# A Fourier-mixing and gated-MLP kernel: the skipped branch without SyncE and VectorE, the last output unit in two halves, and four smaller moves

## The chip, the core and the metric

The kernel runs on one core of a Trainium2 chip. The metric is the device time of one execution in microseconds (us), less is better. The core has five engines that run their own instruction streams and meet at semaphores: TensorE (PE in the profile; PEld are its weight loads), VectorE (DVE), ScalarE (ACT), GpSimd (POOL) and SyncE (SP). SyncE and GpSimd issue DMAs here, which 16 DMA engines carry out.

## What is computed

A token mixing by a two-dimensional Fourier transform and a gated MLP, both of the same x (2048 tokens of 512), are mixed by a sigmoid gate:

```python
def reference(A_x, A_dft_seq_re, A_dft_seq_im, A_dft_hid_re, A_dft_hid_im, B_x, B_w1, B_w3, B_w2, gate_w):
    x = A_x
    g = sigmoid((x * gate_w).sum(-1, keepdims=True))
    a = x @ dft_hid_re.T ;  b = x @ dft_hid_im.T           # over the 512 hidden columns
    y = dft_seq_re @ a - dft_seq_im @ b                    # over the 2048 tokens
    h = silu(x @ w1) * (x @ w3)                            # F = 1376
    return g * y + (1 - g) * (h @ w2)
```

All data are float32. The four DFT matrices are inputs like any other.

## The kernel before

**Arithmetic.** Each float32 operand is split into a high and a low part of a reduced float32 type, and a product is three matmuls (high x high, high x low, low x high; helper at L128). The splits are `high` on ScalarE (L114) and `low` on VectorE (L117).

**Order.** The order is written out by hand: each engine runs its instructions in the order of the code, and a semaphore is waited for where data come from another engine. SyncE's DMAs go out in code order too, one queue over eight semaphore lanes (HW0 to HW7) taken in turn.

**Stages.** After a start of 5.8 us come the gate and up products (to about 207 us): 22 items, each a chunk of 128 of the F columns for one half of the tokens, each item 7 products of 42 matmuls in all (PSUM tiles X, Z and Y; weights `wa` and `wb`). The summed weights `wb` of a chunk are made once, written to DRAM (`wbsp`) and read back by SyncE in two halves ahead of each use (`load_wb`, L206, tiles named wb0_n and wb1_n for weight set n). Then the products with w2 (H, about 207 to 321 us), and the Fourier part in a folded form (321 us to the end). The folded form holds if the DFT matrices have the symmetries of a DFT, and it needs sums and differences of blocks of x ("folds").

**Background tasks.** The folds and the test of the symmetries run beside the products on ScalarE and VectorE. They are tasks in a list; calls of `work` at fixed places of the product loop issue those whose turn it is, by costs that are written beside them, and `load_ahead` issues their loads on SyncE's queue as long as buffers are free. `load_pair` (L661) loads two blocks of x, xr0 and xr7 first. To compare the matrices, blocks `t` of a DFT matrix (16 in each of four groups O1a, O1b, O2, E2) are loaded by SyncE (L728), VectorE takes the difference to a representative block (`differ`, L733 and L735, 128x1024) and ScalarE sums the absolute values (`add_up`, L744). `lone` loads three small pieces with SyncE (L942 to L944) and does some 30 small sums on GpSimd.

**The end.** The Fourier part makes the forms O1, O2 and E2 in PSUM; `even` (L1289) splits each half of E2 into `z_E`, in two pieces of 258 columns for ScalarE and two for VectorE. Then come ten units Y0 to Y9 (L1301). A unit is 12 matmuls into one PSUM tile (6 for the even columns, 128x258, and 6 for the odd ones, 128x256; `chain_two`, L1281), for Y0 to Y5 two updates and for Y6 to Y9 one update of VectorE that reads the tile, scales by the gate and adds the MLP part (L1324, tile r), and one DMA on SyncE's queue to the output (L1325). Units 6 to 9 each give 128 rows of the output.

**The flag and the skipped path.** After unit 3 the sums of the comparison are tested (`verdict`), a matmul of one column adds the 128 results up (`sum_flags`, L576, in front of unit 6), VectorE turns the sum into a flag in SBUF (`see_flags`, L579, behind unit 6's update), and each engine loads the flag into a register (SyncE at L1338, the four others at L1340 behind unit 9). A branch on that register (`tc.If`, L1347) skips a block that computes the Fourier part without any symmetry. With the inputs used here the block is always skipped. An engine that has instructions in the block jumps over them and then, in the else side, brings its semaphores to the values that the block would have left; an engine without instructions in it has nothing to make up. At the end (L1587) SyncE checks its queues' semaphores one by one, drains, and the engines meet at a barrier.

Of the kernel before, what the change touches and what calls it, by code (L numbers as in the profile page):

```python
# [10 lines left out]
AF = mybir.ActivationFunctionType  # L11
# [19 lines left out]
def fnet_swiglu_gate_kernel(  # L31
# [26 lines left out]
    nc = tc.nc  # L58
# [529 lines left out]

    COLD, LAND, TOKENS, RATE, HOLD = [], [4], [1.0], [0.7], [4]
# [11 lines left out]
    def load_ahead(n):  # L601
        thaw()
        for i in ORDER:
            _, _, _, _, f, need, temps = QUEUE[i]
            if i in LOADED:
                continue
            if sum(k not in ISSUED and QUEUE[k][5] > 0 for k in LOADED) >= n or len(F4) < need + temps + min(HELD_BACK[0], HOLD[0]) + RES[0]:
                return
            if f and TOKENS[0] < 0:
                return  # L610
            if f:
                f()
                TOKENS[0] -= need
            HELD_BACK[0] += temps
            LOADED[i] = NOW[0] if f else -99
# [114 lines left out]
    def differ(kind, i):  # L730
        t, r = TR[16 * GROUPS.index(kind) + i], REP[kind]
        if i < 8:
            nc.vector.tensor_sub(t, t, r)  # L733
        elif kind != "E2":
            nc.vector.tensor_add(t, t, r)  # L735
        else:
            im = i > 11
            tv = t.rearrange("p (k n) -> p k n", k=2)
            nc.vector.tensor_tensor(tv, tv, r[:, None, 512 * im : 512 * im + 512].to_broadcast([P, 2, 512]),
                                    op=ALU.add if im else ALU.subtract)  # L740
# [193 lines left out]
    def lone():  # L934
# [7 lines left out]
        nc.sync.dma_start(r0[:1], edges[:, :1024])  # L942
        nc.sync.dma_start(four[:1], edges[:, 1024:1028])
        nc.sync.dma_start(spc, misc[:, :32])  # L944
# [73 lines left out]
    for n in range(SPARE[0], NI):  # L1018
# [5 lines left out]
        do(at_end, n, work, "A", 0.0 if ITEMS[min(n + LOOK, NI - 1)] == (NC - 1, 1) else 1.2)  # L1024
    do(at_end, SPARE[1] - 2, lambda: LIMIT.__setitem__(0, n_gate))
# [263 lines left out]
    def even(p):  # L1289
# [4 lines left out]
        at = [slice(258 * v, 258 * v + 258) for v in range(2)]  # L1294
        for v in range(2):
            high(z[:, 0, at[v]], ps[v])
        for v in range(2):
            low(z[:, 0, at[v]], z[:, 1, at[v]], ps[v])

    even(0)  # L1300
    for u, (kind, za, zb, n, swap) in enumerate(UNITS):  # L1301
# [3 lines left out]
        if u == 6:  # L1305
            sum_flags(ps)

# [3 lines left out]
        evens, odds = (ps[:, lo:hi].rearrange("p (n a) -> p n a", a=2) for lo, hi in ((254, 512), (512, 768)))  # L1311
        chain_two(evens, [(zs(0, za), of_d(0, 0)), (zs(1, zb), of_d(1, 0))])
        chain_two(odds, [(zs(1, za), of_d(0, 1)), (zs(0, zb), of_d(1, 1))])
        r = yp.tile([P, 1024], F32, tag=f"r{u % 6}", name=f"r{u}")
# [5 lines left out]
        for i in range(n):  # L1320
# [3 lines left out]
            nc.vector.scalar_tensor_tensor(rv, src, g_pos[:, k : k + 1], nv, op0=ALU.mult, op1=ALU.add)  # L1324
        nc.sync.dma_start(out[FIRST[u] : FIRST[u] + n].rearrange("k p n -> p k n"),  # L1325
# [10 lines left out]
        if u == 6:  # L1336
            see_flags(ps)
            nc.sync.reg_load(bad_in[mybir.EngineType.SP], seen)  # L1338
    for e in (nc.gpsimd, nc.scalar, nc.tensor, nc.vector):
        e.reg_load(bad_in[e.engine], seen)  # L1340
# [6 lines left out]
    with tc.If(bad > 0, label="other"):  # L1347
# [11 lines left out]
        for q in range(8):  # L1359
            nc.sync.dma_start(xa[q], xs[q])  # L1360
        for k in range(4):
            nc.sync.dma_start(da[k], df[k])
        for b in range(NTB):
            two = [pair_of(k, f"all{b}_{k}") for k in range(4)]
            uv = [[two[2 * v + m // 2][:, 512 * (m % 2) : 512 * (m % 2) + 512] for m in range(4)] for v in range(2)]
            for q in range(8):
                for par in range(2):
                    c = get(pair, "c", 1024)
                    nc.sync.dma_start(c, wf[b, q, par])
# [10 lines left out]
            for j in range(TB // P):  # L1380
# [9 lines left out]
                else:  # L1390
                    nc.sync.dma_start(nb, nbsp[k - 8])
                nc.vector.scalar_tensor_tensor(y, ps, g_pos[:, k : k + 1], nb, op0=ALU.mult, op1=ALU.add)
                nc.sync.dma_start(out[k], y)
# [200 lines left out]
```

## Time and profile before

| | before |
|---|---|
| runs | 356.77, 357.47 and 358.74 us, median 357.47 us |
| the profiled execution | 357.24 us, of it 355.3 us span from the first to the last instruction |
| mean granted TensorE clock | 0.994 |
| busy: TensorE, VectorE, ScalarE, GpSimd | 348.3 (98%), 308.6 (87%), 233.8 (66%), 67.6 us (19%) |
| DMA | 103.04 MB, mean 290 GB/s |

The span is what the profile's times count from; the rest of the time, 1.9 us, lies around it. In a row of the profile, "out<-in" gives the tiles without their numbers, "x7" the count, the number behind a comma the mean of one in ns, and the bracket or the last column how long the engine idled just before and for what. A q behind an engine's name (SPq, POOLq) marks what its sequencer does beside computing: DMA issues, register loads, branches, semaphore checks.

### The profile page before, as it was taken

What the parts mean: (1) busy time and instruction counts of PE and PEld (TensorE: products, weight loads), DVE (VectorE), ACT (ScalarE), POOL (GpSimd) and SP (SyncE); (2) the same over time, 40 slices, a digit from 0 to 9 for tenths busy, and PEclk for the clock granted to TensorE, in tenths of its full rate; (3) what the DMA queues carried; (4) which work ended last, traced back from release to release, by engine and by line L of the source; (5) the groups of instructions that cost most, each with busy time, mean ns of one, the idle gap of its engine ahead of it and who ended that gap; (6) DMA issues with size and microseconds to landing.
All of it is one profiled execution on the core that took longest, in us unless ns stands there. A gap on an engine that the chain in (4) does not pass through costs nothing.

```text
span 355.3 us, 5132 instructions
## 1 busy us (share of the span) xinstructions
PE 348.3 (98%) x1720; PEld 304.5 (86%) x1720; DVE 308.6 (87%) x418; ACT 233.8 (66%) x395; POOL 67.6 (19%) x118
## 2 busy tenths in 40 slices
PE   8999999999999999999999999999999999999993
PEld 4888888888888888888888888888888888889992
DVE  4999989999869788888887799989969979998982
ACT  5875766556648687775433589552588998879930
POOL 0012333333101222111112843421021010000000
PEclk9999999999999999999999999999999999999997
DMA  7648995669636779999999159996659999998184
GB/s 286 245 160 293 351 367 215 221 235 343 214 121 220 213 226 396 400 402 401 365 389 285 52 157 385 406 355 220 223 164 395 404 410 408 409 409 315 59 316 163
DMA packets 33861, 103.04 MB, mean 290 GB/s; under 512 B 5925, under 2 KB 6183, under 8 KB 33832
## 3 DMA queue, kind: packets, MB, share of 16 engines
q1 hardware_dynamic: 26344, 75.93, 57.7%
q0 software_dynamic: 7488, 26.75, 20.3%
q8 instruction: 14, 0.23, 0.3%
q14 instruction: 15, 0.12, 0.1%
HBM read 78.02 MB, written 24.65 MB: 289 GB/s over the span
## 4 chain that ended last, share of the span: by engine, by line
PE 97%; DMA 1%; DVE 0%; issue 0%
PE H L128 32%; PE X L128 31%; PE Z L128 15%; PE Y L128 8%; PE C L128 3%; PE Y L1281 3%; PE O L128 3%; PE wps L416 1%; PE E L128 1%; DMA out<-r 1%; DVE r L1324 0%; PE Y L576 0%
## 5 line engine op out<-in xcount | busy, mean ns | idle before, releaser
L128 PE MATMUL H<-w2t,ht 128*128 128x512 f32 (+1 forms) x528 | 114.1, 379 | 0.0
L128 PEld LDWEIGHTS H<-w2t,ht 128*128 128x128 f32 (+1 forms) x528 | 99.8, 189 | 14.2
L128 PE MATMUL X<-xo,wb 128*128 128x512 f32 x378 | 88.6, 379 | 0.0
L128 PEld LDWEIGHTS X<-xo,wb 128*128 128x128 f32 x378 | 71.4, 189 | 10.2
L744 ACT ACTIVATE t<-t 128x1024 f32<-128x1024 f32 (+1 forms) x68 | 67.4, 994 | 1.5 <-DVE t L733 1.4
L319 POOL DMA_DIRECT2D hs<-h x36 | 19.7, 547 | 88.2 <-DVE h L390 63.4
L401 ACT ACTIVATE h<-X 128x512 f32<-128x512 f32 x21 | 12.5, 596 | 32.0 <-PE X L128 29.9
L733 DVE TENSOR_TENSOR t<-t,rep 128x1024 f32<-128x1024 f32 x28 | 33.1, 1219 | 0.0
L114 ACT ACTIVATE ht<-hr 128x1024 fp32r<-128x1024 f32 x19 | 20.0, 1053 | 18.3 <-PE H L128 10.6
L380 DVE TENSOR_TENSOR u<-u,X 128x512 f32<-128x512 f32 x21 | 14.4, 687 | 20.1 <-PE X L128 12.1
L128 PE MATMUL X<-xo,wa 128*128 128x512 f32 x126 | 30.7, 380 | 0.0
L128 PE MATMUL Z<-xo,wa 128*128 128x512 f32 x126 | 30.6, 379 | 0.0
L128 PE MATMUL Y<-xo,wa 128*128 128x512 f32 x126 | 30.6, 379 | 0.0
L128 PE MATMUL Z<-xo,wb 128*128 128x512 f32 x126 | 30.6, 379 | 0.0
L735 DVE TENSOR_TENSOR t<-t,rep 128x1024 f32<-128x1024 f32 x24 | 28.2, 1219 | 0.0
L128 PEld LDWEIGHTS X<-xo,wa 128*128 128x128 f32 x126 | 23.7, 189 | 3.6 <-DVE wa L117 0.3
L128 PEld LDWEIGHTS Y<-xo,wa 128*128 128x128 f32 x126 | 23.8, 189 | 3.4
L128 PEld LDWEIGHTS Z<-xo,wb 128*128 128x128 f32 x126 | 23.8, 189 | 3.4
L128 PEld LDWEIGHTS Z<-xo,wa 128*128 128x128 f32 x126 | 23.8, 189 | 3.4
L117 DVE TENSOR_TENSOR ht<-hr,ht 128x1024 fp32r<-128x1024 f32 x19 | 23.2, 1219 | 0.1
L117 DVE TENSOR_TENSOR wa<-ws,wa 128x768 fp32r<-128x768 f32 (+1 forms) x22 | 19.3, 880 | 4.0 <-ACT wa L114 3.8
L114 ACT ACTIVATE wa<-ws 128x768 fp32r<-128x768 f32 (+2 forms) x21 | 16.9, 806 | 7.8 <-PE Z L128 6.0
(197 smaller groups left out, 492.5 us busy)
## 6 DMA issues: line engine op xcount, KB each, us to landing
t<-wt SPq DMA_DIRECT2D x60, 512.0 KB, 9.2
hr<-hs SPq DMA_DIRECT2D x19, 512.0 KB, 7.4
hs<-h POOLq DMA_DIRECT2D x36, 256.0 KB, 5.2
wbsp<-wb POOLq DMA_DIRECT2D x16, 512.0 KB, 4.5
wb<-wbsp SPq DMA_DIRECT2D x16, 512.0 KB, 9.5
xs_B<-xt SPq DMA_DIRECT2D x8, 512.0 KB, 3.9
xr<-xw SPq DMA_DIRECT2D x8, 512.0 KB, 13.0
ws<-w POOLq DMA_DIRECT2D x6, 512.0 KB, 5.0
```

Of the source, the lines that this page charges most:

```text
L114: nc.scalar.activation(hi, src, AF.Copy)
L117: nc.vector.tensor_sub(lo, src, hi.bitcast(F32))
L128: nc.tensor.matmul(ps.rearrange("p (n a) -> p n a", a=2), u, turns(v)[:, some], **kw)
L319: nc.gpsimd.dma_start(hs[c][:, b * TB : (b + 1) * TB], h)
L380: nc.vector.tensor_add(u4, u4, x)
L401: nc.scalar.activation(g1, x, AF.Silu)
L416: nc.tensor.matmul(wps, warm[:, :P], warm, start=True, stop=True)
L733: nc.vector.tensor_sub(t, t, r)
L735: nc.vector.tensor_add(t, t, r)
L744: nc.scalar.activation(t[:, :n], t[:, :n], AF.Abs, accum_out=acc[:, i : i + 1])
L1281: nc.tensor.matmul(to, u[i], v[j], start=n == k == 0, stop=n == len(terms) - 1 and k == 2, skip_group_check=True)
```

## The change

- **Skipped path.** In the skipped block, the DMAs go from SyncE to GpSimd's queue, and the last update from VectorE to ScalarE (scaling) and GpSimd (addition). SyncE and VectorE have no instruction left in it.
- **Last unit in halves.** Unit 9's odd columns get a PSUM tile of their own, `Yodd`; its update and its output DMA are done in two halves of 128x256.
- **Flag sooner.** The flag's matmul stands in front of unit 5, `see_flags` in front of unit 5's updates, and SyncE, GpSimd and ScalarE load the register there; TensorE loads it in front of unit 8, VectorE still at the end.
- **O2's differences.** The block differences of group O2 are two VectorE instructions of 128x512 instead of one of 128x1024.
- **Folds of x.** With `PAUSE`, `load_ahead` issues no background load from the middle to the end of the one item in which xr0 and xr7 would be first, so that a load of `wb` goes out ahead of them.
- **Small loads.** The three DMAs of `lone` move to GpSimd's queue.
- **E2's splits** are one piece of 516 columns for each engine and half.

```diff
--- before.py
+++ after.py
@@ -586,6 +586,7 @@
         ORDER.append(len(QUEUE) - 1)
         return ORDER[-1]
 
+    PAUSE = [False]
     COLD, LAND, TOKENS, RATE, HOLD = [], [4], [1.0], [0.7], [4]
 
     def free_later(*tiles):
@@ -600,6 +601,8 @@
 
     def load_ahead(n):
         thaw()
+        if PAUSE[0]:
+            return
         for i in ORDER:
             _, _, _, _, f, need, temps = QUEUE[i]
             if i in LOADED:
@@ -729,7 +732,11 @@
 
     def differ(kind, i):
         t, r = TR[16 * GROUPS.index(kind) + i], REP[kind]
-        if i < 8:
+        if kind == "O2":
+            f = nc.vector.tensor_sub if i < 8 else nc.vector.tensor_add
+            for a in range(2):
+                f(*(v[:, 512 * a : 512 * a + 512] for v in (t, t, r)))
+        elif i < 8:
             nc.vector.tensor_sub(t, t, r)
         elif kind != "E2":
             nc.vector.tensor_add(t, t, r)
@@ -939,9 +946,9 @@
         r0, r1 = ROWS
         for v in (edge_p, er_p):
             g.memset(v.bitcast(F32), 0.0)
-        nc.sync.dma_start(r0[:1], edges[:, :1024])
-        nc.sync.dma_start(four[:1], edges[:, 1024:1028])
-        nc.sync.dma_start(spc, misc[:, :32])
+        nc.gpsimd.dma_start(r0[:1], edges[:, :1024])
+        nc.gpsimd.dma_start(four[:1], edges[:, 1024:1028])
+        nc.gpsimd.dma_start(spc, misc[:, :32])
         a, b = r0[:1, :512], r0[:1, 512:]
         u, v = r1[:1, :512], r1[:1, 512:]
         g.tensor_add(u, a, b)
@@ -1022,6 +1029,8 @@
             do(mid, n, work, "D", 1.7 if n >= SPARE[1] else 1.3 if WSET[n] == WSET[n + 1] else 0.0)
         do(second, n, work, "A", 2.4 if n < NI - 1 else 0.0)
         do(at_end, n, work, "A", 0.0 if ITEMS[min(n + LOOK, NI - 1)] == (NC - 1, 1) else 1.2)
+    do(mid, SPARE[1], PAUSE.__setitem__, 0, True)
+    do(at_end, SPARE[1], PAUSE.__setitem__, 0, False)
     do(at_end, SPARE[1] - 2, lambda: LIMIT.__setitem__(0, n_gate))
 
 
@@ -1291,37 +1300,51 @@
         ps = two[:, :258], two[:, 512:770]
         forms(*ps, ("E2",), range(2), p)
         z = Z["E2", p] = z_E[:, p]
-        at = [slice(258 * v, 258 * v + 258) for v in range(2)]
-        for v in range(2):
-            high(z[:, 0, at[v]], ps[v])
-        for v in range(2):
-            low(z[:, 0, at[v]], z[:, 1, at[v]], ps[v])
+        zh, zl = (z[:, h].rearrange("p (v n) -> p v n", v=2) for h in range(2))
+        split(zh, zl, two.rearrange("p (v n) -> p v n", v=2)[:, :, :258])
 
     even(0)
     for u, (kind, za, zb, n, swap) in enumerate(UNITS):
         if u == 4:
             even(1)
         ps = next_two(f"Y{u}")
-        if u == 6:
+        if u == 5:
             sum_flags(ps)
+        if u == 8:
+            nc.tensor.reg_load(bad_in[mybir.EngineType.PE], seen)
 
         def zs(p, at):
             return [Z[kind, p][:, h, at : at + P] for h in range(2)]
 
-        evens, odds = (ps[:, lo:hi].rearrange("p (n a) -> p n a", a=2) for lo, hi in ((254, 512), (512, 768)))
+        apart = u == len(UNITS) - 1
+        po = next_two("Yodd") if apart else ps
+        evens, odds = (v[:, lo:hi].rearrange("p (n a) -> p n a", a=2)
+                       for v, lo, hi in ((ps, 254, 512), (po, 512, 768)))
         chain_two(evens, [(zs(0, za), of_d(0, 0)), (zs(1, zb), of_d(1, 0))])
         chain_two(odds, [(zs(1, za), of_d(0, 1)), (zs(0, zb), of_d(1, 1))])
+        if u == 5:
+            see_flags(ps)
+            for e in (nc.sync, nc.gpsimd, nc.scalar):
+                e.reg_load(bad_in[e.engine], seen)
         r = yp.tile([P, 1024], F32, tag=f"r{u % 6}", name=f"r{u}")
         nb = NB.pop(u)
 
         def both(v):
             return v.rearrange("p (a m) -> p a m", a=2)[:, :, :256]
 
-        for i in range(n):
+        for i in range(0 if apart else n):
             k = FIRST[u] + i
             rv, nv = (both(v[:, i * D : i * D + D]) for v in (r, nb))
             src = both(ps[:, 255:769])[:, :, ::-1] if i ^ swap else both(ps[:, 254:770])
             nc.vector.scalar_tensor_tensor(rv, src, g_pos[:, k : k + 1], nv, op0=ALU.mult, op1=ALU.add)
+        if apart:
+            k = FIRST[u]
+            for a, src in enumerate((ps[:, 255:511], po[:, 512:768])):
+                at = slice(256 * a, 256 * a + 256)
+                nc.vector.scalar_tensor_tensor(r[:, at], src[:, ::-1], g_pos[:, k : k + 1], nb[:, at],
+                                               op0=ALU.mult, op1=ALU.add)
+                nc.sync.dma_start(out[k][:, at], r[:, at])
+            continue
         nc.sync.dma_start(out[FIRST[u] : FIRST[u] + n].rearrange("k p n -> p k n"),
                           r.rearrange("p (k n) -> p k n", k=2)[:, :n])
         if FIRST[u] > 7:
@@ -1333,11 +1356,7 @@
             work_until(set(range(n_late)))
         if u == 3:
             verdict()
-        if u == 6:
-            see_flags(ps)
-            nc.sync.reg_load(bad_in[mybir.EngineType.SP], seen)
-    for e in (nc.gpsimd, nc.scalar, nc.tensor, nc.vector):
-        e.reg_load(bad_in[e.engine], seen)
+    nc.vector.reg_load(bad_in[mybir.EngineType.DVE], seen)
     bad = nc.snap(bad_in, donate=True, min_val=0, max_val=0x3F800000)
     close(zo_a_cm, lp_cm)
     close(mov_cm, sp_cm, hh_cm, f4d_cm, y_cm)
@@ -1357,16 +1376,16 @@
         xa = [get(gen, f"x{q}", 1024) for q in range(8)]
         da = [get(gen, f"d{k}", 1024) for k in range(4)]
         for q in range(8):
-            nc.sync.dma_start(xa[q], xs[q])
+            nc.gpsimd.dma_start(xa[q], xs[q])
         for k in range(4):
-            nc.sync.dma_start(da[k], df[k])
+            nc.gpsimd.dma_start(da[k], df[k])
         for b in range(NTB):
             two = [pair_of(k, f"all{b}_{k}") for k in range(4)]
             uv = [[two[2 * v + m // 2][:, 512 * (m % 2) : 512 * (m % 2) + 512] for m in range(4)] for v in range(2)]
             for q in range(8):
                 for par in range(2):
                     c = get(pair, "c", 1024)
-                    nc.sync.dma_start(c, wf[b, q, par])
+                    nc.gpsimd.dma_start(c, wf[b, q, par])
                     for v in range(2):
                         for m in range(4):
                             sl = slice(par * D + m * P, par * D + m * P + P)
@@ -1388,9 +1407,10 @@
                 if k < 8:
                     nb = NBK[k // 2][:, k % 2 * D : (k % 2 + 1) * D]
                 else:
-                    nc.sync.dma_start(nb, nbsp[k - 8])
-                nc.vector.scalar_tensor_tensor(y, ps, g_pos[:, k : k + 1], nb, op0=ALU.mult, op1=ALU.add)
-                nc.sync.dma_start(out[k], y)
+                    nc.gpsimd.dma_start(nb, nbsp[k - 8])
+                nc.scalar.activation(y, ps, AF.Copy, scale=g_pos[:, k : k + 1])
+                nc.gpsimd.tensor_add(y, y, nb)
+                nc.gpsimd.dma_start(out[k], y)
         close(gen_cm, pair_cm)
     close(f4_a_cm)
```

The list of an engine's instructions shows where they stand now. A row names the line, the operation, the tiles and the size; x6 stands for six in a row.

SyncE's queue around the first x loads, in the second half of the gate and up products; before:

```order
L728 DMA t47_1342<-wt 128x1024
L661 DMA xr0_1375<-xw 128x1024
L661 DMA xr7_1377<-xw 128x1024
L206 DMA wb1_13_1382<-wbsp_97 128x1024
L206 DMA wb0_14_1413<-wbsp_97 128x1024
L661 DMA xr3_1423<-xw 128x1024
```

and in the changed kernel:

```order
L731 DMA t47_1351<-wt 128x1024
L206 DMA wb1_13_1387<-wbsp_97 128x1024
L664 DMA xr0_1402<-xw 128x1024
L664 DMA xr7_1404<-xw 128x1024
L206 DMA wb0_14_1424<-wbsp_97 128x1024
L664 DMA xr3_1435<-xw 128x1024
```

The half weight wb1_13 has moved ahead of the two x loads; nothing else has changed places there.

TensorE from unit 5 to the branch; before:

```order
L1281 MATMUL Y5_3269<-dt_1944,z_O2_3082 128x258 x6
L1281 MATMUL Y5_3269<-dt_1944,z_O2_3082 128x256 x6
L576 MATMUL Y6_3286<-const-float32-1.0,tail_93 1x1
L1281 MATMUL Y6_3286<-dt_1944,z_E2_3126 128x258 x6
L1281 MATMUL Y6_3286<-dt_1944,z_E2_3126 128x256 x6
L1281 MATMUL Y7_3305<-dt_1944,z_E2_3126 128x258 x6
L1281 MATMUL Y7_3305<-dt_1944,z_E2_3126 128x256 x6
L1281 MATMUL Y8_3321<-dt_1944,z_E2_3126 128x258 x6
L1281 MATMUL Y8_3321<-dt_1944,z_E2_3126 128x256 x6
L1281 MATMUL Y9_3337<-dt_1944,z_E2_3126 128x258 x6
L1281 MATMUL Y9_3337<-dt_1944,z_E2_3126 128x256 x6
L1340 TENSOR_LOAD tail_93
```

and in the changed kernel (tail holds the flag):

```order
L576 MATMUL Y5_3280<-const-float32-1.0,tail_93 1x1
L1290 MATMUL Y5_3280<-dt_1959,z_O2_3097 128x258 x6
L1290 MATMUL Y5_3280<-dt_1959,z_O2_3097 128x256 x6
L1290 MATMUL Y6_3302<-dt_1959,z_E2_3141 128x258 x6
L1290 MATMUL Y6_3302<-dt_1959,z_E2_3141 128x256 x6
L1290 MATMUL Y7_3318<-dt_1959,z_E2_3141 128x258 x6
L1290 MATMUL Y7_3318<-dt_1959,z_E2_3141 128x256 x6
L1314 TENSOR_LOAD tail_93
L1290 MATMUL Y8_3334<-dt_1959,z_E2_3141 128x258 x6
L1290 MATMUL Y8_3334<-dt_1959,z_E2_3141 128x256 x6
L1290 MATMUL Y9_3351<-dt_1959,z_E2_3141 128x258 x6
L1290 MATMUL Yodd_3352<-dt_1959,z_E2_3141 128x256 x6
```

The flag's matmul has moved one unit up, the register load two units, and the odd columns of unit 9 go to their own tile.

SyncE's queue from unit 5's output to the branch; before:

```order
L1325 DMA out<-r5_3282 128x2x512
L1325 DMA out<-r6_3300 128x512
L1338 TENSOR_LOAD tail_93
L1325 DMA out<-r7_3318 128x512
L1325 DMA out<-r8_3334 128x512
L1325 DMA out<-r9_3350 128x512
L1347 COMPARE_AND_BRANCH
L1360 DMA all_x0_3374<-xs 128x1024
```

and in the changed kernel:

```order
L1328 TENSOR_LOAD tail_93
L1348 DMA out<-r5_3298 128x2x512
L1348 DMA out<-r6_3315 128x512
L1348 DMA out<-r7_3331 128x512
L1348 DMA out<-r8_3348 128x512
L1346 DMA out<-r9_3365 128x256 x2
L1366 COMPARE_AND_BRANCH
L1366 UNCONDITIONAL_BRANCH x2
```

The register load has moved ahead of unit 5's output, unit 9's output is two DMAs, and behind the branch nothing of the skipped block is left on SyncE (before, all_x0 is the first of its DMAs there).

## The prediction

> **What bounds the kernel now.** I read the page's busy shares first, then the table of busy time by stretch, then the chain that ended last.
>
> ```profile
> span 355.3 us, 5132 instructions
> PE 348.3 (98%) x1720; PEld 304.5 (86%) x1720; DVE 308.6 (87%) x418; ACT 233.8 (66%) x395; POOL 67.6 (19%) x118
> ...
> core 0: us, PE busy (x) PEld busy (x) DVE busy (x) ACT busy (x) POOL busy (x), PEclk, DMA share, GB/s
> 0.00:5.80 5.80, 4.89 (x12) 1.63 (x12) 0.88 (x3) 2.53 (x5) 0.19 (x4) 1.00 0.59 219
> 5.80:349.30 343.50, 343.45 (x1709) 302.88 (x1709) 306.99 (x416) 231.29 (x391) 67.41 (x114) 1.00 0.80 295
> 349.30:355.30 6.00, 0.00 (x0) 0.00 (x0) 0.74 (x1) 0.00 (x0) 0.00 (x0) 0.67 0.25 91
> ```
>
> From 5.8 to 349.3 us TensorE is busy 343.45 of 343.50 us at the full clock (1.00). The change takes no matmul away, so nothing in that stretch can get shorter; it can only get longer, where a new wait opens. What a change can gain lies in the last 6.0 us, where no matmul runs. These are its rows: the last update of the output (L1324), its DMA (L1325), the flag's register loads (L1340), the branch over the skipped path (L1347) and the closing checks (L1587). A last "350.1 to 350.1" is first and last start.
>
> ```profile
> 349.29 0.75 DVE L1324 SCALAR_TENSOR_TENSOR r<-Y,tail,nbr 128x512 f32<-128x512 f32 x1 [0.59 <-DMA out<-r]
> L1325 SPq DMA_DIRECT2D out<-r x1: 853/853/853, 350.1 to 350.1; - x1
> DMA to landing us min/median/max: 3.1/3.1/3.1
> ...
> L1347 SPq COMPARE_BRANCH  x1: 70/70/70, 351.0 to 351.0; - x1
> L1347 SPq EVENT_SEMAPHORE  x1: 17/17/17, 352.1 to 352.1; - x1
> L1347 SPq EVENT_SEMAPHORE  x2: 17/17/17, 353.2 to 353.3; - x2
> L1347 SPq EVENT_SEMAPHORE  x5: 17/17/17, 353.4 to 353.6; - x5
> L1587 SPq EVENT_SEMAPHORE  x12: 28/28/28, 353.7 to 354.4; - x12
> L1587 SPq DRAIN  x1: 7/7/7, 354.5 to 354.5; - x1
> ```
>
> The last DMA is issued at 350.1 and lands 3.1 us later, at 353.2, which is when SyncE's second check passes. Behind it stand 6 more checks of this kind and 12 closing ones, some 65 ns apart, up to the drain at 354.5; the barrier among the engines then takes 0.8 us to 355.3. So the end is: last matmul, last update, last landing, 18 checks one by one, barrier.
>
> **The change part by part.** *Last unit in halves.* Unit 9's even and odd columns now go to separate PSUM tiles, so half of the update needs only the even matmuls. Each half is 128x256.
>
> ```profile
> L1281 PE MATMUL Y<-dt,z_E x21: 274/275/276, 346.7 to 349.0; 128*128 128x256 f32 x12, 128*128 128x258 f32 x9
> L1324 DVE SCALAR_TENSOR_TENSOR r<-Y,tail,nbr x8: 742/747/751, 342.3 to 349.3; 128x512 f32<-128x512 f32 x8
> L117 DVE TENSOR_TENSOR z_E<-E,z_E 128x258 fp32r<-128x258 f32 x4 | 1.5, 419 | 0.6 <-ACT z_E L114 0.6
> L230 DVE TENSOR_TENSOR wu<-wu,ws 128x256 f32<-128x256 f32 x11 | 4.7, 425 | 0.4
> L405 DVE TENSOR_TENSOR h<-h,u 128x512 f32<-128x512 f32 x21 | 14.4, 686 | 2.5 <-ACT h L401 2.5
> ```
>
> The 12 matmuls of 128x256 are the odd halves of units 8 and 9; six take some 0.7 us, so the even half of unit 9 is done at 348.6 and the first half-update ends before 349.1, beside the odd matmuls. The second half starts at 349.3 as before. Bounds for it: 0.42 (the 258-column row out of PSUM) and 0.49 (747 less 686 minus 425, what 256 columns cost between two plain rows); I take 0.45 instead of 0.75, so the second DMA is issued at 349.8, 0.3 earlier. The first half's issue at 349.1 is out of its way: issues take 0.33 (L206, below) to 0.85 (L1325).
>
> How long does 128 KB take to land? The trace has no such store. The nearest are the 256 KB ones:
>
> ```profile
> DMA to landing us min/median/max: 2.5/2.5/2.5
> DMA to landing us min/median/max: 3.3/3.3/3.3
> q8 instruction: 14, 0.23, 0.3%
> q14 instruction: 15, 0.12, 0.1%
> ```
>
> The first is that of units 6 and 7 (345 to 347.5), the second that of unit 8 (348.7). 128 KB less are 0.3 us at 399 GB/s (the rate of the stretch 142.31 to 151.37, quoted below). So 2.2 to 3.0, that is a landing at 352.0 to 352.8; I take 2.5, between the 2.2 of an undisturbed store and the 2.8 of the last one (3.1 less 0.3), so 352.3 instead of 353.2: 0.9 us, with 0.4 and 1.2 as ends. What lengthens the last two stores the views don't name. Code fetches share the 16 engines: 14 of 16 KB in q8 at 0.3% of 16 engines' span are some 1.2 us each on one engine (0.003 x 16 x 355.3 / 14), and a store has landed only when its slowest engine has. [...]
>
> *Skipped path.* SyncE and VectorE have nothing in the skipped block any more, so the else side no longer makes up their semaphores: the 8 checks of SyncE at L1347 and one of VectorE go. The 12 closing checks stay, but the lanes are checked in the order 0 to 7; with three loads fewer and one store more on SyncE's queue, unit 9's second half sits on lane 7, the last one checked. The 11 before it run while it is in flight: SyncE issues at 349.8, is free at 350.1 to 350.7, and needs 0.1 for the branch and 0.7 for 11 checks, so 350.9 to 351.5, before 352.0. After the landing one check and the drain are left, 0.1 us instead of 1.3 (353.2 to 354.5): 1.2 us gained. If the last landing fell on lane 0 instead, 11 checks of 62 ns would be left and the gain 0.5.
>
> ScalarE and GpSimd take the work over, GpSimd with 214 instructions to step over instead of 1, then 5 checks and one bulk update.
>
> ```profile
> L1347 POOLq COMPARE_BRANCH  x1: 53/53/53, 347.3 to 347.3; - x1
> L1587 POOLq DRAIN  x3: 40/107/323, 347.5 to 355.1; - x3
> L1581 POOLq INC_SWDGE_SEM  x1: 27/27/27, 0.1 to 0.1; - x1
> L1340 POOLq TENSOR_LOAD <-tail x1: 1104/1104/1104, 346.1 to 346.1; - x1
> L1340 PEldq TENSOR_LOAD <-tail x1: 796/796/796, 347.1 to 347.1; - x1
> 343.58 0.12 PE Y L576 x2
> ```
>
> Bounds for its step: 0.2 (its own, 347.3 to 347.5) and 1.1 (SyncE's 351.0 to 352.1 over 168 instructions, part of which is its wait for unit 8's store). It branches at 345.0 now, so its cover is 7 us up to the landing; zero on the path. [...]
>
> *Flag sooner.* The flag's matmul (0.12 us ahead of unit 6, the last row above, from the chain) moves to unit 5, its comparison stands before unit 5's update (one number, on VectorE, which idles 0.59 before the last update and waits there for matmuls, so that a delay in unit 5 is made up). ScalarE, GpSimd and SyncE load it at about 343.9; a load takes 0.8 to 1.1 us by the two rows above, so SyncE has it at 344.7 to 345.0, about when unit 5's store is due, and that store has 7 us in hand. TensorE's load stands before unit 8, so 24 matmuls queue behind it. In the old trace its load began at 347.1 while matmuls went on to 349.25: the sequencer is 2.1 us ahead. A load of 0.8 leaves 1.3: zero, above it at most the 0.8.
>
> *O2's differences in halves.* 15 on VectorE, each 1219 ns in one piece:
>
> ```profile
> L733 DVE TENSOR_TENSOR t<-t,rep 128x1024 f32<-128x1024 f32 x28 | 33.1, 1219 | 0.0
> 99.00:160.00 61.00, 61.00 (x284) 53.33 (x283) 50.05 (x69) 42.25 (x76) 11.44 (x21) 1.00 0.79 284
> L380 DVE TENSOR_TENSOR u<-u,X 128x512 f32<-128x512 f32 x7 | 4.8, 686 | 10.0 <-ACT t L744 4.4 <-PE X L128 3.2 <-ACT wa L114 2.4
> ```
>
> Two of 686 are 0.15 more each, 2.3 us in all. VectorE has 61.00 less 50.05 us idle there, 10.0 of it in front of L380, the only update that TensorE waits for soon. Zero; upper end 2.3.
>
> *First x loads behind weights.* wb1_13 now goes out ahead of xr0 and xr7 (1 MB).
>
> ```profile
> L206 SPq DMA_DIRECT2D wb<-wbsp x1: 326/326/326, 142.5 to 142.5; - x1
> DMA to landing us min/median/max: 5.4/9.2/12.0
> 155.26 1.46 PE L128 MATMUL X<-xo,wb 128*128 128x512 f32 x6
> 142.31:151.37 9.06, 9.06 (x43) 7.94 (x42) 7.45 (x10) 6.59 (x12) 1.68 (x4) 1.00 1.02 399
> L665 DVE TENSOR_TENSOR xp<-xr,xr x2: 1218/1218/1218, 162.0 to 163.1; 128x1024 f32<-128x1024 f32 x2
> xr<-xw SPq DMA_DIRECT2D x8, 512.0 KB, 13.0
> ```
>
> wb1_13 is issued at 142.5, wanted at 155.26, and the slowest of the nine wb loads from 133 to 170 takes 12.0 (the second row): some 0.8 us to spare in this execution, and perhaps none in another. Without 1 MB ahead of it, it lands up to 2.6 us sooner (1 MB at 399 GB/s). That is worth 0 here and 0 to 0.3 in a median. VectorE reads the x loads at 162.0, and such a load takes 13.0 in the median of 8. They go out a few us later, behind the weights: how much later the planner's hold decides, but the stretch from 142.3 to 151.4 is the one at full DMA rate, and a late one stops VectorE (which has the 10.0 of idle time named above), not TensorE. Zero.
>
> *Small loads to GpSimd's queue; E2's splits in one piece.* GpSimd's sums may start later by the time of a load, some 4 to 5 us by the shortest landing above; before its last copies GpSimd is idle for 9.7 us, waiting for VectorE, so up to that much is made up. Of E2's splits ScalarE and VectorE each do one piece of 516 columns instead of two of 258, beside unit 0 and unit 4's matmuls. Zero both.
>
> ```profile
> L879 POOL COPY xo_O1a<-row 1x256 f32<-1x256 f32 x1 | 3.1, 3132 | 9.7 <-DVE xo_O1a L685 9.7
> ```
>
> **Sum.** 0.9 + 1.2 = 2.1 us off the profiled execution's 357.24 (span 355.3 and 1.9 around it): 355.1, span 353.2. The median of the runs, 357.47, lies 0.23 above it: 355.3. About 0.5% (1.8 us) is what a measurement of this kernel can tell from no change.
>
> **Rivals.** *The landing hardly moves.* The code fetch or the long issue (853 ns) falls on the second half's DMA: landing at 352.8, gain 0.4 + 1.2, or less where SyncE's checks are then late: 355.7 to 356.3. For it: both last stores are slow by 0.6 to 0.8. Against it: the halves give the first one 0.6 us of head start.
>
> *TensorE stops at the load.* If its queue held less than the load takes, or the flag came late, 0.8 to 1.1 us of the 2.1 go: 356.2 to 356.5. Against: the 2.1 us of lead.
>
> *GpSimd is last at the barrier (slower).* Its way over 214 instructions and the bulk update lasts beyond the landing; every us beyond 352.3 is one lost, and from 9.4 us (345.0 to 354.4) the kernel is slower than before: 357.5 to 359. For: the update's cost on the else side is not in the trace except as 27 ns at the start. Against: 1.1 us is the longest step over a block that is.
>
> **How the numbers follow.** The forecast 0.62 (354.4 to 355.6), the landing 0.26, TensorE's stop 0.07, GpSimd 0.05. Faster by over 0.5% is the first alone, 0.62; within it the next two, 0.33; slower 0.05. The range runs from 354.3 (3.0 gained, the best landing and a weight wait removed) to 356.8, which takes in the second and third cases and the spread of the medians.
>
> **What would show it.** Right: SyncE has no L1366 semaphore rows but goes from its branch to closing checks that mostly lie before the last landing; one check, a drain and 0.8 us of barrier follow; two stores of 128 KB at 349.1 and 349.8; TensorE still ends at 349.3. Wrong: a gap in TensorE's row near 344 to 346; GpSimd's drain after 352; a second store that lands after 352.8.

## The result and the profile after

The changed kernel takes 355.83 us (median of 9 runs, 355.14 to 356.26), the kernel before 357.47 us (median of 9, 356.75 to 358.86). The ratio is 0.995, with a 95% interval of 0.9931 to 0.9968: 1.6 us less by the medians, 1.8 by the ratio, and between 1.1 and 2.5 by its interval. The forecast was 355.3, and 354.3 to 356.8.

The page of the changed kernel, its first two lines, and the table of busy time by stretch (the second stretch from the end of the last matmul on):

```profile
span 354.0 us, 5144 instructions
PE 348.4 (98%) x1720; PEld 303.6 (86%) x1720; DVE 309.9 (88%) x432; ACT 233.8 (66%) x393; POOL 68.9 (19%) x121
10.50:342.80 332.30, 332.30 (x1631) 292.30 (x1629) 299.15 (x413) 228.27 (x384) 68.70 (x117) 1.00 0.79 293
342.80:349.90 7.10, 7.10 (x64) 6.86 (x62) 5.58 (x10) 0.00 (x0) 0.00 (x0) 1.00 0.78 289
349.94:354.10 4.16, 0.00 (x0) 0.00 (x0) 0.48 (x1) 0.00 (x0) 0.00 (x0) 0.83 0.37 131
```

From 10.5 us to its last matmul TensorE is never idle, as before. The last matmul ends at 349.93 instead of 349.25. Of that 0.7 us, 0.5 is already there at the matmul that starts at 10.8 instead of 10.3 us, behind two waits of TensorE (0.19 and 0.38 us) for ScalarE's splits of the first inputs; path_alone below, which changes nothing there, is 0.5 us late at that place, too. The rest comes in one step at 146 us, for which the views name no wait. So the two profiles are compared from the end of the last matmul: from there to the end it was 6.09 us, and it is 4.11.

The timeline of this stretch (start, length, engine), unit 9's two stores by their line, and SyncE's branch and closing checks:

```profile
349.30 0.48 DVE L1344 SCALAR_TENSOR_TENSOR r<-Y,tail,nbr 128x256 f32<-128x256 f32 x1
349.97 0.48 DVE L1344 SCALAR_TENSOR_TENSOR r<-Yodd,tail,nbr 128x256 f32<-128x256 f32 x1 [0.18 <-PE Yodd L1290]
L1346 SPq DMA_DIRECT2D out<-r x2: 392/628/864, 349.8 to 350.8; - x2
DMA to landing us min/median/max: 2.3/2.6/2.9
L1366 SPq COMPARE_BRANCH  x1: 64/64/64, 351.2 to 351.2; - x1
...
L1607 SPq EVENT_SEMAPHORE  x9: 27/28/28, 351.4 to 351.9; - x9
...
L1607 SPq EVENT_SEMAPHORE  x1: 28/28/28, 353.1 to 353.1; - x1
L1607 SPq DRAIN  x1: 7/7/7, 353.2 to 353.2; - x1
```

SyncE goes from its branch straight to the 12 closing checks. Nine of them run while the stores are in flight, two wait for unit 8's store and for the first half, and the last one (353.1) waits for the second half, which lands at 353.07. One drain and the barrier follow: 0.97 us from the last landing to the end, where it was 2.16. The last landing itself comes 3.14 us after the last matmul's end, where it was 3.92.

The halves did not run as thought: the first store's issue took 864 ns, and the second, whose data were ready at 350.46, was issued only at 350.79.

GpSimd's way over the skipped block and TensorE's register load, the two things that could have cost time:

```profile
L1366 POOLq COMPARE_BRANCH  x1: 53/53/53, 345.4 to 345.4; - x1
L1366 POOLq EVENT_SEMAPHORE  x5: 17/43/43, 345.8 to 346.2; - x5
L1366 POOLq INC_SWDGE_SEM  x1: 247/247/247, 346.3 to 346.3; - x1
L1314 PEldq TENSOR_LOAD <-tail x1: 1057/1057/1057, 345.1 to 345.1; - x1
L1328 SPq TENSOR_LOAD <-tail x1: 478/478/478, 344.8 to 344.8; - x1
```

GpSimd is through at 346.6, 6.5 us before the last landing, and in the table above TensorE is busy for 7.10 of the 7.10 us around its load.

### The profile page after: what moved, and what is told of

The parts are those of the page before. It is cut to its first block, busy times and chain, and to the rows that moved or that the text cites. A ratio compares the mean times of both kernels' runs of the same rounds, so it can differ in the third digit from the quotient of the medians.

```text
span 354.0 us, 5144 instructions
## 1 busy us (share of the span) xinstructions
PE 348.4 (98%) x1720; PEld 303.6 (86%) x1720; DVE 309.9 (88%) x432; ACT 233.8 (66%) x393; POOL 68.9 (19%) x121
## 4 chain that ended last, share of the span: by engine, by line
PE 97%; DMA 2%; SPq 0%; DVE 0%; ACT 0%; issue 0%
PE H L128 32%; PE X L128 31%; PE Z L128 15%; PE Y L128 8%; PE Y L1290 4%; PE O L128 3%; PE C L128 3%; DMA ws<-w 2%; PE E L128 1%; PE Yodd L1290 0%; DVE r L1344 0%; ACT a L114 0%; SPq L173 0%; SPq L197 0%; PE Y L576 0%
## 5 line engine op out<-in xcount | busy, mean ns | idle before, releaser
L128 PEld LDWEIGHTS X<-xo,wb 128*128 128x128 f32 x378 | 71.3, 189 | 10.5 <-issue 0.3
L740 DVE TENSOR_TENSOR t<-t,rep 128x1024 f32<-128x1024 f32 x21 | 24.7, 1220 | 0.0
L738 DVE TENSOR_TENSOR t<-t,rep 128x512 f32<-128x512 f32 x30 | 19.0, 684 | 0.0
```

Of the source, the lines that this page charges most:

```text
L128: nc.tensor.matmul(ps.rearrange("p (n a) -> p n a", a=2), u, turns(v)[:, some], **kw)
L738: f(*(v[:, 512 * a : 512 * a + 512] for v in (t, t, r)))
```

## The experiments

Each kernel is the one before or the changed one with some parts done or undone. The times are medians; the ratio is to the kernel before, run on the same chip. A time says little below 1 us here, so the traces were read beside them, and the table behind the experiments puts what they showed side by side.

**One part at a time.** First the two parts that the forecast's sum is made of.

The skipped block alone was changed (all its DMAs move as the first one does):

```diff
-            nc.sync.dma_start(xa[q], xs[q])
+            nc.gpsimd.dma_start(xa[q], xs[q])
...
-                nc.vector.scalar_tensor_tensor(y, ps, g_pos[:, k : k + 1], nb, op0=ALU.mult, op1=ALU.add)
+                nc.scalar.activation(y, ps, AF.Copy, scale=g_pos[:, k : k + 1])
+                nc.gpsimd.tensor_add(y, y, nb)
```

> The kernel before with the skipped block alone changed (no SyncE and VectorE in it). Theory (what counts is how many checks stand behind the last landing): unit 9's one store lies on lane 1 of 8, so behind its landing 6 closing checks of 62 ns and the drain are left, 0.45 us, where the kernel before had 1.26: 0.8 us less, about 356.7. Rival (the else side is worth its whole length, whatever the lane): 1.2 us less, about 356.2. The landing itself stays 3.1 us after its issue.

Measured: 356.94 us, ratio 0.9987 (0.9967 to 1.0008). In its trace the last landing is followed by 6 checks, and 1.33 us pass from it to the end instead of 2.16: 0.83 us, as the theory with the lanes has it. The time alone can't tell it from no change.

Unit 9 alone was put in halves, as in the changed kernel (L1320 and L1340 to L1347 there):

```diff
+        po = next_two("Yodd") if apart else ps
...
+                nc.sync.dma_start(out[k][:, at], r[:, at])
```

> The kernel before with unit 9 in two halves alone. Theory: the last landing comes 0.8 us sooner (measured against the last matmul) and falls on lane 6, so 1 check of the else side and 12 closing ones follow, 0.85 us instead of 1.26: about 1.2 us less in all, 356.3. Rival (SyncE's long issue of 0.85 us falls on the first half and takes the gain back): 0.3 to 0.5 less, 357.0.

Measured: 357.78 us, ratio 1.002 (0.9997 to 1.0044): nothing gained. The forecast's second term is not there. Its two stores, and the DMA rows of the 1.3 us window 350.4 to 351.7, in which TensorE fetches a block of code (queue q8):

```profile
L1334 SPq DMA_DIRECT2D out<-r x2: 383/973/1563, 350.5 to 352.1; - x2
DMA to landing us min/median/max: 2.6/3.2/3.8
q8 instruction: 1, 0.02, 5.7%
```

5.7% of 16 engines and 1.3 us are 1.19 us for one packet: in the trace's DMA records it runs from 350.45 to 351.64. The first store's issue starts at 350.45, too, and lasts until 352.01. So the second half goes out 1.56 us after the last matmul's end (350.55), later than a whole store would have (0.82), and lands at 4.11 us, where the whole store of the kernel before landed at 3.92. Nor did the checks behind it shrink as expected: the last store lies on lane 2, and not on lane 6, and 2.08 us follow it instead of 2.16.

Both parts were done together:

> The kernel before with both. Theory: the second half lands on lane 2, so 5 closing checks follow, 0.38 us: 0.8 + 0.9 = 1.7 us less, about 355.8, nearly all that the whole change brings. Rival (the five small moves carry part of the gain): no more than 1.0 to 1.3 less.

Measured: 357.24 us, ratio 0.9982 (0.9964 to 0.9999): 0.5 to 0.6 us less, and not the 1.7 of the theory. So the five small moves, which the forecast had at zero, carry part of the gain. The trace gives two reasons. One is again the first store's issue, 1.39 us. The other is a wait of TensorE (its waits between 150 and 165 us, and the group of matmuls that had it):

```profile
PE X L128 <- DMA wb<-wbsp: 1.7, 1, 1.7
L128 PE MATMUL X<-xo,wb 128*128 128x512 f32 x18 | 4.3, 383 | 1.7 <-DMA wb<-wbsp 1.7
```

TensorE waits 1.7 us for wb1_13, the weight that the change sends ahead of the x loads.

> The changed kernel with the skipped block and unit 9 as before, so that only the five small moves are left (flag sooner, O2's differences in halves, x loads behind the weight, small loads on GpSimd's queue, E2's splits in one piece). Theory: no difference, 357.2 to 357.7, and TensorE goes from 10 us to the end in the same time within 0.1 us. Rival: the weight load that had 0.8 us to spare was late in some executions: up to 0.3 less in the median. Second rival: TensorE's register load in front of unit 8 stops it: 0.8 more.

Measured: 357.36 us, ratio 0.9973 (0.9947 to 0.9999). There is a gain, if only just clear of zero, about as much as from the two large parts together. Which of the five has it was tried next.

**Weight and flag.** `PAUSE` was tried alone, the flag's three edits alone, and each of them on top of path_and_halves.

The weight's place is set in `load_ahead` and in the product loop:

```diff
+        if PAUSE[0]:
+            return
...
+    do(mid, SPARE[1], PAUSE.__setitem__, 0, True)
+    do(at_end, SPARE[1], PAUSE.__setitem__, 0, False)
```

> The kernel before with one of the small moves alone: wb1_13 goes out ahead of the loads of xr0 and xr7. In the profile of path_and_halves TensorE stood 1.9 us in front of the product with wb1_13, in halves_alone 0.3, in path_alone 0.1, in the kernel before 0. Theory A: this weight's 0.8 us to spare is too little in many executions, and the move takes the wait away: 0.4 to 0.9 us less in the median, and no execution far above the others from that cause. Rival B (the flag's place carries the gain of the small moves): no difference.

The flag's place is set among the units:

```diff
+        if u == 5:
+            sum_flags(ps)
+        if u == 8:
+            nc.tensor.reg_load(bad_in[mybir.EngineType.PE], seen)
...
+        if u == 5:
+            see_flags(ps)
+            for e in (nc.sync, nc.gpsimd, nc.scalar):
+                e.reg_load(bad_in[e.engine], seen)
...
```

> The kernel before with the flag sooner alone. SyncE's issue of unit 9's store has ended 0.37 to 0.39 us after the end of TensorE's 16 KB code fetch in all profiles so far in which the two overlap. Theory A: no difference in the median (up to 0.3 less). Rival B: TensorE's branch, and so its code fetch, comes sooner against the last store, the issue is short and the store lands sooner: 0.4 to 0.9 less.

> The skipped block, unit 9 in halves and wb1_13 ahead of the x loads. Theory A: 0.4 to 0.9 us less than path_and_halves, so 356.4 to 356.9 beside 357.7 of the kernel before; the first half's issue still takes 1.4 to 1.6 us, since TensorE's code fetch starts 0.2 us after its last matmul's start. Rival B: as path_and_halves, 0.5 less than before.

> The skipped block, unit 9 in halves and the flag sooner. Theory: TensorE's code fetch starts some 0.5 us sooner against its last matmul than in path_and_halves, so the first half's issue takes 0.9 instead of 1.4 us and the second half lands 0.5 us sooner: 0.5 less than path_and_halves. Rival A alone (the flag does nothing): as path_and_halves. If the flag carried all of the small moves' gain, 1.1 less than path_and_halves.

Measured: pause_alone 357.41 us, ratio 0.9981 (0.9956 to 1.0007); flag_alone 356.90, 0.9974 (0.9947 to 1.0001); both_pause 356.52, 0.9955 (0.993 to 0.998); both_flag 356.56, 0.9975 (0.9948 to 1.0003). Singly, no interval leaves out zero. Of the two on top of path_and_halves, only both_pause is clearly faster than the kernel before. Of the 0.5 us below path_and_halves that were expected of both_flag, the ratios show 0.25 and the medians 0.7, and the noise leaves it open.

For the weight the traces say more. In the six kernels that were profiled with the old order, wb1_13 landed 12.2 to 13.7 us after its issue, and TensorE waited in three of them (0.2 us in halves_alone, 0.7 in both_flag, 1.7 in path_and_halves). In the eight kernels with the new order it was 10.0 to 10.9 us, and in none of the eight did TensorE wait there. The executions agree: of 149 of the kernels with the old order, 16 lay over 1.3 us above their own median, of 70 with the new order none (one cause among others for such executions, so this supports it and does not prove it).

For the flag, the trace of flag_alone has TensorE's last code fetch from 0.56 us before to 0.77 us after the last matmul's end, where the kernel before had it from 0.10 before to 1.30 after. The last store's issue, 0.82 us after that matmul, took 853 ns before and is short now (here the last three stores of flag_alone, all short):

```profile
L1331 SPq DMA_DIRECT2D out<-r x3: 333/335/344, 347.2 to 349.9; - x3
```

The store lands at 3.51 instead of 3.92 us: 0.4 us that the forecast had not given to the flag. It isn't all the flag's, though: in path_alone, with the late flag but a fetch of 0.99 instead of 1.40 us, the store lands at 3.43, and in both_flag the second half lands at 3.97, later than in path_and_halves (3.81).

**The halves in the changed kernel, and the code fetch.** What are the halves worth where the flag is sooner? They were undone, given one store for both, issued by ScalarE, and run with the code shifted.

The changed kernel was given unit 9 as before (the update and the store are whole again, too):

```diff
-        apart = u == len(UNITS) - 1
-        po = next_two("Yodd") if apart else ps
...
```

> The changed kernel with unit 9 whole again (one update, one store). In all profiles so far an issue of SyncE that falls into TensorE's last code fetch ends 0.37 to 0.39 us after that fetch. Theory (the halves' first store is issued inside the fetch, 0.1 us before the last matmul's end, and holds up the second): the whole store is issued 0.82 us after the last matmul, behind the fetch, in 0.33 us, and lands at 3.4 to 3.5; one check more stands behind it: 4.4 to 4.6 us from the last matmul to the end (the changed kernel's profile: 4.1, and 5.2 with the flag sooner, both parts and a longer fetch): 355.7 to 356.3, so the halves are worth 0.3 or less. Rival (halves are worth 0.8 as forecast): 4.9 us, 356.6.

One store was put behind both updates:

```diff
-                nc.sync.dma_start(out[k][:, at], r[:, at])
+            nc.sync.dma_start(out[k], r[:, :512])
```

> The changed kernel with unit 9's update in halves, but one store for both. Theory: the store is issued 0.52 us after the last matmul; if the fetch is over by then it takes 0.33 us, if not it ends 0.37 us after the fetch; landing at 3.0 to 3.4, 4.0 to 4.5 us from the last matmul to the end: 355.4 to 356.0. Rival (the second half's smaller size counts): slower than the changed kernel by 0.3.

Both stores were issued by ScalarE:

```diff
-                nc.sync.dma_start(out[k][:, at], r[:, at])
+                nc.scalar.dma_start(out[k][:, at], r[:, at])
```

> The changed kernel with both halves' stores issued by ScalarE. Theory A (TensorE's code fetch holds up an issue of any engine): ScalarE's first issue ends 0.37 us after the fetch, as SyncE's did, and the time is that of the changed kernel, 355.8. Rival B (only SyncE's queue is held up): both issues take 0.33 to 0.4, the second starts at 0.5 us after the last matmul and lands at 2.7; 3.7 us to the end: 355.4.

More code was put ahead of everything (WARM is 11):

```diff
-    for n in range(WARM):
+    for n in range(30):
+        nc.tensor.matmul(wps[:1, :1], warm[:, :1], warm[:, :1], start=True, stop=True)
+    for n in range(WARM - 4):
         nc.tensor.matmul(wps, warm[:, :P], warm, start=True, stop=True)
```

> The changed kernel with 30 matmuls of one column and 7 wide ones as warm-up instead of 11 wide ones, so that TensorE's program is 26 matmuls (52 instructions) longer ahead of everything else. Theory A (the last fetch is that of the jump over the skipped block): it starts 0.56 us before the last matmul's end as before, the first half's issue is held up, and the time is that of the changed kernel. Rival B (the fetch comes every so many instructions): it starts 2 to 3 us sooner, the issues take 0.33 to 0.4, the second half lands at 2.7 after the last matmul: 0.4 to 0.5 us less.

Measured: after_whole 355.92 us, ratio 0.9935 (0.9918 to 0.9951); after_one_store 355.96, 0.9938 (0.9919 to 0.9957); after_act 356.24, 0.9946 (0.993 to 0.9963); after_more_code 356.25, 0.9947 (0.9927 to 0.9967). All four overlap the changed kernel's 0.995 (0.9931 to 0.9968): undoing the halves costs nothing that can be measured, and none of the four beats it clearly. The issues of unit 9's stores, in this order (after_whole: units 8 and 9):

```profile
L1337 SPq DMA_DIRECT2D out<-r x2: 332/344/356, 349.3 to 350.6; - x2
L1346 SPq DMA_DIRECT2D out<-r x1: 759/759/759, 350.2 to 350.2; - x1
L1346 ACTq DMA_DIRECT2D out<-r x2: 377/476/575, 349.2 to 349.9; - x2
L1348 SPq DMA_DIRECT2D out<-r x2: 387/760/1132, 351.3 to 352.5; - x2
```

A whole store goes out behind the fetch, in 356 ns; one store issued earlier (0.55 us after the last matmul) runs into the fetch and loses it again (it lands at 3.65 us, where 3.0 to 3.4 were expected); the first half with the shifted code is held for 1132 ns.

In after_more_code the earlier code fetches came sooner (the first at 15.9 instead of 23.1 us), but the last one started 0.58 us before the last matmul's end, as in the changed kernel (0.55). So it isn't set by the number of instructions ahead of it (rival B would have had it 2 to 3 us sooner); it follows TensorE's branch over the skipped block, 0.75 to 0.78 us behind its end in the six profiles with the late flag, 1.17 to 1.20 in six of the eight with the early one (1.5 in after_act, 1.8 in small_moves_alone).

ScalarE's issues fit neither theory: the first took 377 ns although it started 0.15 us into a fetch (-0.27 to 0.68 us), which speaks against A; the second took 575 ns and ended at 1.13 us, 0.45 us after that fetch's end, which speaks against B.

**All profiles side by side**, from the traces' records, in us from the end of the last matmul: TensorE's last 16 KB code fetch; SyncE's issue that meets it, or unit 9's own (start, length, end; in after_act both of ScalarE's); the last landing; from there to the end; the sum of these two.

| kernel | fetch | issue: start, length, end | last landing | then | sum |
|---|---|---|---|---|---|
| before | -0.10 to 1.30 | 0.82, 0.85, 1.67 | 3.92 | 2.16 | 6.09 |
| path_alone | -0.07 to 0.92 | 0.82, 0.47, 1.29 | 3.43 | 1.33 | 4.76 |
| pause_alone | -0.10 to 1.32 | 0.82, 0.87, 1.69 | 4.05 | 2.16 | 6.21 |
| flag_alone | -0.56 to 0.77 | 0.82, 0.34, 1.15 | 3.51 | 2.16 | 5.67 |
| small_moves_alone | 0.05 to 0.99 | 0.82, 0.56, 1.38 | 3.72 | 1.79 | 5.52 |
| halves_alone | -0.10 to 1.09 | -0.10, 1.56, 1.46 | 4.11 | 2.08 | 6.20 |
| path_and_halves | -0.10 to 0.92 | -0.10, 1.39, 1.29 | 3.81 | 1.27 | 5.08 |
| both_pause | -0.11 to 1.29 | -0.10, 1.76, 1.66 | 4.21 | 1.27 | 5.47 |
| both_flag | -0.56 to 0.63 | -0.10, 1.11, 1.01 | 3.97 | 1.27 | 5.24 |
| changed kernel | -0.55 to 0.39 | -0.10, 0.86, 0.77 | 3.14 | 0.97 | 4.11 |
| after_whole | -0.56 to 0.79 | 0.82, 0.36, 1.17 | 3.51 | 1.03 | 4.55 |
| after_one_store | -0.56 to 0.93 | 0.55, 0.76, 1.31 | 3.65 | 1.03 | 4.69 |
| after_act | -0.27 to 0.68 | -0.12, 0.38, 0.26; 0.56, 0.57, 1.13 | 3.42 | 0.97 | 4.39 |
| after_more_code | -0.58 to 0.65 | -0.10, 1.13, 1.03 | 3.40 | 0.97 | 4.37 |

Two columns go together: wherever SyncE's issue in the table starts before the fetch ends, it ends 0.37 to 0.39 us after the fetch, whatever its own start. Where it starts behind it (flag_alone, after_whole), it takes 0.34 to 0.36. But lying inside the fetch is not enough. Unit 8's issue, at -0.52, starts just behind the beginning of an early fetch and is not held (0.33 us), while the first half's issue in halves_alone, path_and_halves and both_pause starts with a late fetch and is.

The 13 earlier fetches in each trace help to tell what decides. In the 14 profiles together, 117 issues of SyncE start inside one of the 16 KB fetches, the last ones included. For 51 of them SyncE's issue before had ended over 0.3 us ahead of the fetch: all 51 took the usual 0.33 to 0.39 us. For the other 66 it had ended later, or inside the fetch: 58 of these ended 0.36 to 0.43 us after the fetch, six were long without ending there, and two took the usual time. So it is the second issue that is held, counted from about 0.3 us ahead of the fetch's beginning. Unit 9's first half is that second issue, behind unit 8's.

The column "then" is the lane: 0.97 with the last store on the lane checked last, 1.03 with one check more, 1.27 with five more, 1.33 with six, and 1.79 to 2.16 with SyncE's own 8 checks.

## Why the prediction was right, and where its working was not

- **The time and the sum.** 2.1 us were forecast off the profiled execution, and from the last matmul to the end the profiles differ by 1.98: 0.78 in the last landing (forecast 0.9) and 1.19 behind it (forecast 1.2). The median, 355.83, lies above the 354.4 to 355.6 to which the forecast gave a chance of 0.62, and within the 355.7 to 356.3 of the rival in which the landing hardly moves.
- **Skipped path, 1.2: right, with its mechanism.** The 8 checks are gone and the last landing sits on the last lane. path_alone gives 0.83, since its store lies on lane 1; the other 0.3 to 0.4 come from the lane, which the number of SyncE's DMAs sets (three loads fewer, one store more). The forecast's price for a wrong lane (a gain of 0.5 on lane 0, with 11 checks left) had the right price of a check, 62 ns, but a wrong count: four closing checks stand ahead of lane 0, so 7 would be left there, as lane 1 leaves 6.
- **Last unit in halves, 0.9: the step that failed.** It put the first half's issue "out of its way", with 0.33 to 0.85 us for an issue. But 0.85 from -0.10 ends at 0.75, and the second half is ready at 0.52. The issue falls into TensorE's last code fetch as the second one, behind unit 8's, and is held in all six kernels where SyncE issues halves: 0.86 to 1.76 us instead of 0.33. Their worth is nothing with the late flag (halves_alone), 0.37 in the changed kernel's profile with a short fetch (3.14 against after_whole's 3.51), 0.11 with a longer one (after_more_code, 3.40), less than nothing in both_flag (3.97 against flag_alone's 3.51), and nothing in the times. The second half's 128 KB store, issued behind the fetch, took 2.3 to 2.9 us to land (2.28 in the changed kernel, 2.87 in both_flag), as the bounds (2.2 to 3.0) had it.
- **Flag sooner, zero: mis-sized, and its size is open.** It moves TensorE's branch 0.9 us ahead against the last matmul, and with it the code fetch 0.46 us (flag_alone). A whole store's issue then ends at 1.15 to 1.17 us (flag_alone, after_whole) instead of 1.29 to 1.69 (the three with the late flag), so 0.1 to 0.5 sooner, by how long the fetch takes. No landing shows it free of the fetch's length. TensorE did not stop at its load, as forecast: 1057 ns of it were covered.
- **x loads behind the weight, 0 and 0 to 0.3 in a median: too low.** The profiled execution was one without the wait; 0.55 us between landing and use was the spare time, and other executions were 0.2 to 1.7 us short of it. What it is worth in the median stays between 0.4 us (pause_alone, by the medians) and 1.0 (both_pause against path_and_halves, by the ratios), neither resolved by itself.
- **O2's differences, small loads, E2's splits: zero.** O2's 30 halves take 684 ns each, as costed, and TensorE waits for none of them. In the changed kernel's profile GpSimd waits 1.6 us for its row and has its 9.7 us idle later as before. But in small_moves_alone, after_whole and after_one_store, where it waits 2.3 to 2.5 us, VectorE's L390 at 202 us takes 1.20 us instead of 0.69 beside GpSimd's small sums, ScalarE's L368 comes late behind it, and TensorE starts its next product 0.3 to 0.5 us late. So the small loads can cost something; that the later sums are the cause was not tested, and the three parts were not tried one by one.
- **The rivals.** The landing's rival had the right actors, the code fetch and the long issue, with the second half as their victim; it is the first half that they hold. GpSimd was through 6.5 us early.

So the total came out in part by luck. What the halves did not bring in the times, other parts did: by the ratios path_and_halves is 0.6 us faster than the kernel before, both_pause, with the weight, 1.6, and the changed kernel 1.8. Neither the weight's share nor the flag's is resolved by itself. And the profile that agrees so well had one of the shortest last fetches of all, 0.95 us, where they took up to 1.49.

## What to carry to other kernels

A part costed at zero because "it only moves" can move something that collides: list what each engine fetches or issues around the end, and look at whether a store's issue falls into it as the second one (unit 9's first half did in six kernels, and its issue took 0.86 to 1.76 us instead of 0.33). Before the last store is split, set the end of the first piece's issue against the time at which the second piece is ready: in the changed kernel they were 0.77 and 0.52 us after the last matmul, and in the times the split gained nothing. And one profiled execution shows the spare time of a wait in that execution only: with 0.55 us to spare on a landing of 12 us, count the wait as present in some of the runs.

## What the runs showed of the hardware

The 16 KB code fetches in queue q8 are taken as TensorE's, since they move when code is put ahead in TensorE's program (the first from 23.1 to 15.9 us in after_more_code). In these traces such a fetch holds up the second DMA issue of SyncE, counted from 0.3 us ahead of the fetch's beginning, until 0.36 to 0.43 us after its end (58 of 66 issues), while the first takes its usual 0.33 to 0.39 us (51 of 51). In after_act ScalarE's first issue inside a fetch was not held (377 ns), although SyncE's unit 8 had gone out just before; its second took 575 ns. A fetch is one packet of 16 KB (the changed kernel's last one 0.95 us long), and the stores landed with the slowest of their 16 engines: in the changed kernel's trace unit 8's store has 15 of 16 engines done at 1.78 us after the last matmul's end and lands with the last at 2.56; in the trace of the kernel before, 15 are done at 1.52 and it lands at 2.78. Whether the late engine is the one that carries the fetch, and how a fetch comes to hold up the second issue, no run shows. In after_more_code the last fetch stays with TensorE's branch, 0.58 us before the last matmul's end, while the earlier ones move.

The register load took 464 to 499 ns on SyncE, GpSimd and ScalarE when the three loaded at 344.8, and 1057 ns on TensorE at 345.1; in the kernel before the same loads took 796 to 1104 ns.
